# A fused attention, Fourier mix and MLP kernel: two rows of quarter products taken in turn, smaller pieces of w1's operands, and the operands made later

## The chip, the cores and the metric

The kernel runs on one core of one Trainium2 chip. The metric is the device time of one execution in microseconds (us), as the median of several runs; of the kernel before there are three, 1423.19, 1426.36 and 1426.65 us. A traced execution of the same kernel took 1424.23 us, and the traced span from its first to its last instruction is 1422.4 us. All times of stages, waits and instructions are from that one execution.

## The reference

Chunked softmax attention over 8 batches, then a two-dimensional Fourier transform of which the real part is kept, a layer norm, and an MLP with a ReLU between two products:

```python
scores = scale * np.matmul(q_c, k_c.transpose(0, 1, 2, 4, 3))
attn = softmax(scores)                      # per chunk of 64 tokens
x = np.matmul(attn, v_c)                    # bridged to (8, 576, 512)
mixed = np.real(np.fft.fft(np.fft.fft(x, axis=1), axis=2))
u = x + mixed
un = (u - mean) / np.sqrt(var + 1e-06)
out = u + np.maximum(un @ w_ch1, 0.0) @ w_ch2
```

Inputs are q, k and v of 8 x 8 x 576 x 64, w_ch1 of 512 x 2048 and w_ch2 of 2048 x 512, computed in float32. The weights arrive as float64.

## The kernel before

The 4608 tokens are cut into 36 tiles of 128, and these into nine groups of four (`groups`, 512 tokens each): groups 0 to 7 hold the four tiles of one batch, group 8 the leftover chunks of all batches. Each group passes through the MLP as a **first product** (w1, with ReLU into `h1`, 16 rows of 128 features) and a **second product** (w2, with the residual, to the output). The attention and Fourier transform of the next batch run as side work: `side(b)` is a generator, and so is the MLP of a group; the driver at the end (L842 to L866) takes one step `t` of the MLP, then as many steps of the side work as are due by a straight line in `t`. Everything stands in the program in that order (a manual schedule), and each engine works through its own instructions in program order.

Group 0 uses plain products (`mlp_first`, L606): 64 matmuls of 128x512 for each of the two. The groups from 1 on use seven half-size products in place of eight (a Strassen-like scheme, `mlp`, L649): the operands of w1 and w2 are sums and differences of quarters, made once, kept in DRAM as `s1` and `s2` (L95, L96) and streamed back for every group.

- **Making them.** `keep1` (L564) makes four sums of w1's quarters by four GpSimd instructions (L573) into `yall` and stores seven operands with seven DMAs (L576); it is called four times. `keep2` (L578) does it for w2 (L588, L591). The list `conv` (L840, L849) calls one of them per step inside group 0: `keep1` from the step on where more than 16 weight pieces have been rounded, `keep2` once all 32 are through.
- **Rounding.** `load_weight` and `round_weight` (L226 to L258) bring the float64 weights in 32 pieces of 512 KB, 16 of w1 (`wa`) and 16 of w2 (`wb`), and turn each into float32 by four VectorE instructions (L243, L245, L252, L253), three of ScalarE and one of GpSimd (L254).
- **First product, half-size.** One row `m` of eight is a pair of feature blocks. Its seven quarter products (0 to 6, called o0 to o6 below) are two 128x256 matmuls each (L674), into two PSUM tiles `pa` and `pb` of a bank each. After each of them ScalarE (L680, L691) or VectorE (L682, L684, L686, L693, L696) reads the result; the program makes the next product into the same tile wait for that read. `operands(m - 1)` (L659) makes `xs` and `ys` for the second product. The step yields after o3 and after o6.
- **Operands of w1.** `slab1` holds three slabs of 896 KB in `wa`, each with all seven operands of one row. After a row is used, `fetch(1)` (L596, L601) issues the DMA for the row three further on; `fetch(2)` does it for w2's slabs of 1024 KB, one for each quarter product.
- **Second product, half-size.** For each of seven quarter products, two halves of eight matmuls (L727).

Names of the side work: `att_T` transposes q and k (`pt`, L264; ScalarE L274, GpSimd L276 and VectorE L281 write `qT` and `kT`), `att_S` forms scores (`sc`, L293; VectorE L302, L304, L312, L313, L314 and ScalarE L310), `att_P` and `att_V` the weighted sum (`xp`, L331), `fold` and `fourier` the transform (`z`, `mix`). All loads and stores but a few go through SyncE's queue (SP), which issues them in program order and waits there for the engines that they depend on. Each float32 matmul of the program is two records in the trace.

## Time and profile before

| | |
|---|---|
| median of three runs | 1426.36 us |
| the profiled execution, and its span | 1424.23 us, 1422.4 us |
| group 0: first product begins, second begins, group ends | 80.95, 157.43, 298.8 us |
| first product, groups 1 to 8 | 83.4, 83.2, 83.3, 83.2, 83.3, 82.3, 67.6, 67.6 us |
| second product, groups 1 to 8 | 64.9, 66.0, 64.9, 66.0, 65.0, 59.7, 50.1, 53.2 us |

The stages are taken from the first matmul of each on the timeline. Side work runs beside groups 0 to 6; groups 7 and 8 have none in the first product. The lines quoted below have these forms. A group of instructions: line, engine, operation, tiles written and read, sizes, count, then busy time, mean ns of one, and idle time of the engine just before them with what ended it. A timeline row: start, length, engine, instruction, and in brackets the idle time before it with its releaser. A window row: bounds, length, busy time and count of PE, PEld, DVE, ACT and POOL, then the granted TensorE clock, the share of the DMA engines and GB/s. PE is TensorE, PEld its weight load, DVE VectorE, ACT ScalarE, POOL GpSimd, SP SyncE.

### The profile page before, as it was taken

To read this page: it belongs to the slowest core of one execution; us is meant where nothing else is said; L and a number is where in the kernel's file an instruction comes from. 1 tells how busy PE (TensorE), PEld (TensorE's weight loads), DVE (VectorE), ACT (ScalarE), POOL (GpSimd) and SP (SyncE) were. 2 spreads that over 40 slices of the span, in tenths; PEclk is the share of its full clock that TensorE was granted. 3 is DMA by queue.
4 is the path that set the end of the run, shared out by engine and by line. 5 is a ranking of instruction groups with operands and counts; after the bars stand their busy time and mean duration, and the time that the engine had idled before them with its cause. 6 is when DMAs were issued, how large, how long until landed. Compare 5 with 4: busy or idle time off the path is not lost.

```text
span 1422.4 us, 18460 instructions
## 1 busy us (share of the span) xinstructions
PE 1223.7 (86%) x7244; PEld 901.1 (63%) x7244; DVE 587.0 (41%) x1224; ACT 296.3 (21%) x661; POOL 308.6 (22%) x370
## 2 busy tenths in 40 slices
PE   7797348987998889988997899879988998899898
PEld 5443124455687658755785578656865686587577
DVE  4589732444344434434344335432534243313321
ACT  3455511122211211122112211221112101200210
POOL 0338462100330123003200222021303030130121
PEclk9999769999999999999999999999999999999999
DMA  9537665065335433544255425542352234335212
GB/s 214 139 104 222 199 193 127 10 192 191 108 134 171 120 102 110 173 123 134 85 167 150 131 87 140 164 134 89 134 163 83 104 118 141 106 139 174 104 53 95
DMA packets 164028, 189.43 MB, mean 133 GB/s; under 512 B 119461, under 2 KB 137382, under 8 KB 156774
## 3 DMA queue, kind: packets, MB, share of 16 engines
q1 hardware_dynamic: 162150, 187.84, 43.2%
q8 instruction: 57, 0.93, 0.3%
q10 hardware_dynamic: 1600, 0.39, 0.2%
q14 instruction: 29, 0.24, 0.1%
q0 software_dynamic: 192, 0.02, 0.0%
HBM read 163.94 MB, written 24.12 MB: 132 GB/s over the span
## 4 chain that ended last, share of the span: by engine, by line
PE 73%; DVE 13%; ACT 5%; issue 3%; DMA 3%; POOL 3%; SPq 1%; POOLq 0%; ACTq 0%; DVEq 0%
PE pb L674 18%; PE pb L727 16%; PE pa L727 12%; PE pa L674 11%; PE pt L264 4%; PE z L441 3%; PE mix L484 3%; DVE wa L684 2%; DVE h L693 2%; PE dn L625 2%; DVE power L245 2%; DMA xall<-in_moe_w_ch_dram 2%; ACT wa L680 1%; PE xp L331 1%; PE sc L293 1%
## 5 line engine op out<-in xcount | busy, mean ns | idle before, releaser
L663 POOL TENSOR_TENSOR h<-h 128x256 f32<-128x256 f32 x64 | 57.6, 901 | 691.8 <-DVE wb L661 458.3
L674 PE MATMUL pb<-wa 128*128 128x256 f32 x512 | 138.1, 392 | 40.1 <-DVE h L693 40.1
L674 PE MATMUL pb<-unT,wa 128*128 128x256 f32 x512 | 138.1, 392 | 33.1 <-DVE wa L684 33.1
L674 PEld LDWEIGHTS pb<-wa 128*128 128x128 f32 x512 | 92.0, 189 | 75.7 <-DVE h L693 65.8
L674 PE MATMUL pa<-unT,wa 128*128 128x256 f32 x512 | 136.6, 389 | 0.0
L674 PEld LDWEIGHTS pb<-unT,wa 128*128 128x128 f32 x512 | 91.9, 189 | 68.8 <-DVE wa L684 58.8
L727 PE MATMUL pa<-wb,h 128*128 128x256 f32 x512 | 115.6, 381 | 0.0
L727 PE MATMUL pb<-wb,h 128*128 128x256 f32 x512 | 115.1, 381 | 0.0
L674 PE MATMUL pa<-wa 128*128 128x256 f32 x256 | 72.4, 405 | 42.6 <-ACT wa L680 42.6
L727 PEld LDWEIGHTS pa<-wb,h 128*128 128x128 f32 x512 | 95.8, 190 | 16.2 <-issue 3.8
L727 PEld LDWEIGHTS pb<-wb,h 128*128 128x128 f32 x512 | 95.6, 190 | 12.7
L674 PEld LDWEIGHTS pa<-unT,wa 128*128 128x128 f32 x512 | 90.7, 190 | 16.4 <-issue 5.0
L674 PEld LDWEIGHTS pa<-wa 128*128 128x128 f32 x256 | 43.3, 189 | 71.6 <-ACT wa L680 68.3
L682 DVE TENSOR_TENSOR wa<-pa,wa 128x256 f32<-128x256 f32 x64 | 27.2, 424 | 122.4 <-PE pa L674 122.4
L613 PE MATMUL up<-unT,wa 128*128 128x512 f32 x128 | 59.8, 629 | 16.7 <-ACT h L620 15.8
L625 PE MATMUL dn<-wb,h 128*128 128x512 f32 x128 | 63.3, 642 | 0.8 <-ACT h L620 0.8
L691 ACT ACTIVATE h<-pa 128x256 f32<-128x256 f32 x64 | 24.4, 382 | 168.7 <-PE pa L674 168.7
L686 DVE TENSOR_TENSOR h<-pb,wa 128x256 f32<-128x256 f32 x64 | 27.1, 423 | 78.3 <-PE pb L674 78.3
L696 DVE TENSOR_TENSOR h<-pb,wa 128x256 f32<-128x256 f32 x64 | 27.1, 423 | 78.3 <-PE pb L674 78.3
L727 PE MATMUL pa<-wb,yall 128*128 128x256 f32 x256 | 58.2, 381 | 0.0
L727 PE MATMUL pb<-wb,yall 128*128 128x256 f32 x256 | 57.9, 381 | 0.0
L613 PEld LDWEIGHTS up<-unT,wa 128*128 128x128 f32 x128 | 25.7, 203 | 50.3 <-issue 30.6
(148 smaller groups left out, 1818.5 us busy)
## 6 DMA issues: line engine op xcount, KB each, us to landing
wa<-s SPq DMA_DIRECT2D x64, 896.0 KB
wb<-s SPq DMA_DIRECT2D x56, 1024.0 KB
xall<-in_moe_w_ch_dram SPq DMA_DIRECT2D x32, 512.0 KB
v<-in_v_dram SPq DMA_DIRECT2D x142, 64.0 KB
s<-yall SPq DMA_DIRECT2D x32, 256.0 KB
q<-in_q_dram SPq DMA_DIRECT2D x34, 128.0 KB
k<-in_k_dram SPq DMA_DIRECT2D x34, 128.0 KB
q<-in_q_dram SPq DMA_DIRECT2D x14, 256.0 KB
```

What stands on the lines that cost most here:

```text
L245: nc.vector.tensor_scalar(p, hi, 0x7FF00000, None, ALU.bitwise_and)
L264: nc.tensor.transpose(pt[:, j, :], src(j), ident)
L441: nc.tensor.matmul(out=z[:, 0:NQ], lhsT=pm[p, fold_, half], rhs=tk[p, i, fold_, :], start=(i == 0), stop=(i == NM), skip_group_check=(T == 2),
L484: nc.tensor.matmul(out=o[:, cols], lhsT=zt[:, T], rhs=tab, start=(T == 0), stop=(T == 3), skip_group_check=True,)
L613: nc.tensor.matmul(out=up, lhsT=w1[:, kk, m * 128:(m + 1) * 128], rhs=unT[:, kk], start=(kk == 0), stop=(kk == KD - 1),)
L625: nc.tensor.matmul(out=dn, lhsT=h1[:, m, s * 128:(s + 1) * 128], rhs=w2[:, m, :], start=(m == 0), stop=(m == KF - 1),)
L663: nc.gpsimd.tensor_tensor(out=h1[:, m, hi], in0=h1[:, m, lo], in1=h1[:, m, hi], op=ALU.subtract)
L674: nc.tensor.matmul(out=out_, lhsT=w[:, o, kk], rhs=rhs[:, kk], start=(start and kk == 0), stop=(kk == 1), skip_group_check=True,)
L682: nc.vector.tensor_tensor(out=b, in0=pa[:, 1], in1=a, op=ALU.add)
L684: nc.vector.tensor_tensor(out=a, in0=pb[:, 0], in1=b, op=ALU.add)
L693: nc.vector.tensor_tensor(out=h1[:, m, hi], in0=pb[:, 0], in1=b, op=ALU.add)
L727: nc.tensor.matmul(out=dst, lhsT=lhs[:, m], rhs=w[:, m], start=(start and m == 0), stop=(m == HF - 1), skip_group_check=True,)
```

## The change

- **Two rows in turn.** The first product's half-size form (`up_halves`) now takes rows in pairs: o0 of both rows, o1 of both rows, and so on, with `pa` and `pb` for each of the two rows (the same four PSUM banks). It yields after o1, o3, o5 and o6 of a pair, four times as before per two rows. `operands` for the pair before follow o3.
- **Smaller pieces.** `s1` is laid out by pair and quarter product. `slab1` is ten pieces of 256 KB, one for each quarter product of a pair, where it was three slabs of 896 KB; a fetch follows every quarter product. The bytes of a group are the same, in 28 DMAs where there were 8.
- **Operands made later.** `keep1` moves from group 0 to the first eight steps of group 1, `keep2` stays after the last rounded piece; both are generators now, taken three and two small steps per step of the MLP, and `keep1` uses `yall` and `os_` (in `wb`) by turns.
- **Group 1.** Since w1's operands are not there yet, group 1's first product is plain (`up_plain`), with `operands` made behind it; its second product is half-size as before.

```diff
+    s1 = dram.tile([HF // 2, NO, 128, 2 * 2 * 128], FP32, name="s1")
+    NS1, NS2, Z1, Z2 = 10, 3, 2 * 2 * 128, HF * HM
+    slab1 = [wa[:, i * Z1:(i + 1) * Z1].rearrange("p (k r f) -> p k r f", r=2, k=2) for i in range(NS1)]
-    def keep1(f, kk):
+    def keep1(i):
+        f, kk = divmod(i, 2)
...
-        o1, o2, o3, o4 = (yall[:, i] for i in range(4))
+        o1, o2, o3, o4 = ((os_ if i % 2 else yall)[:, j] for j in range(4))
...
             nc.gpsimd.tensor_tensor(out=out_, in0=in0, in1=in1, op=op)
+            yield
+        to = s1.rearrange("a o p (k x) -> p a o k x", k=2)[:, 2 * f:2 * f + 2]
         for o, a in enumerate((a11, o2, o1, o3, a12, o4, a22)):
+            nc.sync.dma_start(out=to[:, :, o, kk], in_=a.rearrange("p (a x) -> p a x", a=2))
+        yield
...
+    first_of = {1: 2, 2: 1}
     def fetch(which):
         i = n_slab[which]
+        if which == 1 and i < HF // 2 * NO * (NG - first_of[1]):
+            pair, o = divmod(i % (HF // 2 * NO), NO)
+            nc.sync.dma_start(out=slab1[i % NS1].rearrange("p k r f -> p (k r f)"), in_=s1[pair, o])
...
+    def up_plain(g):
...
             nc.scalar.activation(out=h1[:, m], in_=up, func=ACTF.Relu)
+            if g >= first_of[2] and m > HF:
+                operands(h1, m - HF - 1)
+            yield h1
...
+    def up_halves(g):
+        rhs = (unT[:, 0:2, lo], tt[:, 1], tt[:, 0], unT[:, 0:2, hi], unT[:, 2:4, lo], unT[:, 2:4, hi], tt[:, 2])
+        for pair in range(HF // 2):
+            pas, pbs = {}, {}
+            for o in range(NO):
+                w = slab1[((g - first_of[1]) * HF // 2 * NO + pair * NO + o) % NS1]
+                for r in range(2):
+                    m = 2 * pair + r
+                    a, b = tmp[:, r, 0], tmp[:, r, 1]
+                    if o == 0:
+                        pas[r] = ps_f.tile([128, 2, 256], FP32, tag="ff", name="pa")
+                    if o == 2:
+                        pbs[r] = ps_f.tile([128, 2, 256], FP32, tag="ff", name="pb")
+                    dst = (pas, pas, pbs, pbs, pas, pbs, pbs)[o][r][:, (0, 1, 0, 1, 0, 0, 1)[o]]
+                    for kk in range(2):
+                        nc.tensor.matmul(
+                            out=dst, lhsT=w[:, kk, r], rhs=rhs[o][:, kk],
+                            start=(o in (0, 2) and kk == 0), stop=(kk == 1), skip_group_check=True,
+                        )
+                    if o == 0:
+                        nc.scalar.copy(a, dst)
+                    elif o == 1:
+                        nc.vector.tensor_tensor(out=b, in0=dst, in1=a, op=ALU.add)
...
+                    elif o == 3:
+                        nc.vector.tensor_tensor(out=h1[:, HF + m, hi], in0=dst, in1=a, op=ALU.add)
+                        if pair > 0:
+                            operands(h1, m - 2)
...
+                fetch(1)
+                if o in (1, 3, 5, 6):
+                    yield h1
...
-                if g == 0 and conv and n_w > (KD * KF // 4 if len(conv) > HF // 2 else len(pieces)):
-                    conv.pop(0)()
+                if n_w > len(pieces):
+                    for _ in range(2):
+                        next(conv2, None)
                 if t == begin[1] - 1:
-                    while conv:
-                        conv.pop(0)()
-                    for _ in range(NS):
+                    for _ in conv2:
+                        pass
+                if begin[1] <= t < begin[1] + KF // 2:
+                    for _ in range(3):
+                        next(conv1, None)
+                if t == begin[1] + KF // 2:
+                    for _ in range(NS2):
+                        fetch(2)
+                if t == begin[1] + KF:
+                    for _ in range(NS1):
                         fetch(1)
```

In the changed file the lines have moved: the first product's matmuls are L690 there, `keep1`'s GpSimd instructions L575, `keep2`'s L592, the rounding's L255.

TensorE at the start of group 2's first product, before (tiles of the program carry numbers, so that the two rows can be told apart):

```order
L674 MATMUL pa_2829<-unT_2570,wa_90 128x256 x2
L674 MATMUL pa_2829<-wa_90 128x256 x2
L674 MATMUL pb_2830<-wa_90 128x256 x2
L674 MATMUL pb_2830<-unT_2570,wa_90 128x256 x2
L293 MATMUL sc_2843<-kT_2746,qT_2739 64x64 x16
L674 MATMUL pa_2829<-unT_2570,wa_90 128x256 x2
L674 MATMUL pb_2830<-unT_2570,wa_90 128x256 x2
L674 MATMUL pb_2830<-wa_90 128x256 x2
L264 MATMUL pt_2881<-ident_81,q_2748 128x128 x4
L264 MATMUL pt_2888<-ident_81,k_2751 128x128 x4
L674 MATMUL pa_2901<-unT_2570,wa_90 128x256 x2
L674 MATMUL pa_2901<-wa_90 128x256 x2
```

The same place in the changed kernel:

```order
L690 MATMUL pa_2716<-unT_2457,wa_90 128x256 x2
L690 MATMUL pa_2720<-unT_2457,wa_90 128x256 x2
L690 MATMUL pa_2716<-wa_90 128x256 x2
L690 MATMUL pa_2720<-wa_90 128x256 x2
L294 MATMUL sc_2732<-kT_2633,qT_2626 64x64 x16
L690 MATMUL pb_2758<-wa_90 128x256 x2
L690 MATMUL pb_2762<-wa_90 128x256 x2
L690 MATMUL pb_2758<-unT_2457,wa_90 128x256 x2
L690 MATMUL pb_2762<-unT_2457,wa_90 128x256 x2
L265 MATMUL pt_2774<-ident_81,q_2635 128x128 x4
L265 MATMUL pt_2781<-ident_81,k_2638 128x128 x4
L690 MATMUL pa_2716<-unT_2457,wa_90 128x256 x2
```

Before, o0 and o1 of a row stand next to each other and write one tile (`pa_2829`); now o0 and o1 of one row (`pa_2716`) have a product of the other row (`pa_2720`) between them, and the step of the side work that forms scores (`sc`) has moved from behind o3 to behind o1.

GpSimd from the last rounded pieces of w1 to the first copies of `qT` of batch 1's attention, before (`yall<-wa` and `yall<-yall,wa` are `keep1`, `yall<-wb` is `keep2`):

```order
L573 TENSOR_TENSOR yall<-wa 128x512
L573 TENSOR_TENSOR yall<-wa,yall 128x512
L254 TENSOR_TENSOR wb<-wb,power 128x512 x11
L588 TENSOR_TENSOR yall<-wb 128x512
L588 TENSOR_TENSOR yall<-wb,yall 128x512
L588 TENSOR_TENSOR yall<-wb 128x512
L588 TENSOR_TENSOR yall<-wb,yall 128x512
L588 TENSOR_TENSOR yall<-wb 128x512
L588 TENSOR_TENSOR yall<-wb,yall 128x512
L588 TENSOR_TENSOR yall<-wb 128x512
L588 TENSOR_TENSOR yall<-wb,yall 128x512
L276 COPY qT<-qT 128x8 x2
```

And in the changed kernel:

```order
L255 TENSOR_TENSOR wa<-wa,power 128x512 x10
L255 TENSOR_TENSOR wb<-wb,power 128x512 x16
L592 TENSOR_TENSOR yall<-wb 128x512
L592 TENSOR_TENSOR yall<-wb,yall 128x512
L592 TENSOR_TENSOR yall<-wb 128x512
L592 TENSOR_TENSOR yall<-wb,yall 128x512
L277 COPY qT<-qT 128x8 x2
L592 TENSOR_TENSOR yall<-wb 128x512
```

The sixteen instructions of `keep1` between the pieces of w2 (four of them in the first rows above) are gone from here, and four instead of eight of `keep2` stand ahead of `qT`.

GpSimd later, in group 1 of the changed kernel, where the same instructions now stand:

```order
L500 TENSOR_TENSOR xall<-y,xall 128x513 x2
L277 COPY qT<-qT 128x8 x2
L575 TENSOR_TENSOR yall<-wa 128x512
L575 TENSOR_TENSOR yall<-yall,wa 128x512
L575 TENSOR_TENSOR yall<-wa 128x512
L350 MEMSET xall 128x1
L575 TENSOR_TENSOR yall<-wa,yall 128x512
L575 TENSOR_TENSOR wb<-wa 128x512
L575 TENSOR_TENSOR wb<-wb,wa 128x512
L575 TENSOR_TENSOR wb<-wa 128x512
L575 TENSOR_TENSOR wb<-wa,wb 128x512
```

The copies of `qT` for batch 2's first tiles stand ahead of `keep1`, and its sums go by turns into `yall` and into `os_` (in `wb`).

More of the change, by code (lines that the diff above doesn't have):

```diff
@@ L582, in keep2 @@
         b21, b22 = w2[:, HF + m:HF + m + 2, 0:HM], w2[:, HF + m:HF + m + 2, HM:DM]
[L583 removed]
+        o1, o2, o3, o4 = (yall[:, j].rearrange("p (m e) -> p m e", m=2) for j in range(4))
         for out_, in0, in1, op in (
@@ L639, in mlp_first @@
                             turned(g + 1, j)
-                            if j >= 2:
+                            if j >= 2 and g + 1 >= first_of[1]:
                                 combined(g + 1, j - 2)
@@ L728, in mlp @@
                         out=dst, lhsT=lhs[:, m], rhs=w[:, m],
-                        start=(start and m == 0), stop=(m == HF - 1), skip_group_check=True,
+                        start=(o in (0, 2) and m == 0), stop=(m == HF - 1), skip_group_check=True,
                     )
@@ L772, in mlp @@
                 yield
+    def mlp(g):
+        for h1 in (up_halves if g >= first_of[1] else up_plain)(g):
+            yield
+        yield from (down_halves if g >= first_of[2] else down_plain)(g, h1)
     with tc.manual_schedule():
@@ L837, with chain @@
         for g in range(NG):
-            begin.append(begin[-1] + (KF + G * PARTS if g == 0 else 2 * HF + 2 * NO))
-        ready_at = [begin[g] + (KF + G * PARTS - 6 if g == 0 else 2 * HF + 4) for g in range(NG)]
-        conv = [lambda f=f, kk=kk: keep1(f, kk) for f in range(2) for kk in range(2)]
-        conv += [lambda i=i: keep2(i) for i in range(HF // 2)]
+            begin.append(begin[-1] + (KF if g < first_of[1] else 2 * HF) + (G * PARTS if g < first_of[2] else 2 * NO))
+        ready_at = [begin[g] + (KF + G * PARTS - 6 if g < first_of[2] else 2 * HF + 4) for g in range(NG)]
+        conv2 = iter([step for i in range(HF // 2) for step in [keep2(i)]])
+        conv1 = iter([step for i in range(4) for step in [keep1(i)]])
+        def chain(gens):
+            for gen in gens:
+                yield from gen
+        conv2, conv1 = chain(conv2), chain(conv1)
         t = 0
         for g in range(NG):
-            for _ in (mlp(g) if g else mlp_first(g)):
+            for _ in mlp(g):
                 t += 1
```

135 lines of the change are left out of this document (50 added, 85 removed).

## The prediction

> **What bounds the kernel now.** I read the page first: its busy times, the granted clock, the chain that ended last, and the groups that waited.
>
> ```profile
> PE 1223.7 (86%) x7244; PEld 901.1 (63%) x7244; DVE 587.0 (41%) x1224; ACT 296.3 (21%) x661; POOL 308.6 (22%) x370
> PEclk9999769999999999999999999999999999999999
> PE 73%; DVE 13%; ACT 5%; issue 3%; DMA 3%; POOL 3%; SPq 1%; POOLq 0%; ACTq 0%; DVEq 0%
> L674 PE MATMUL pb<-unT,wa 128*128 128x256 f32 x512 | 138.1, 392 | 33.1 <-DVE wa L684 33.1
> L674 PE MATMUL pb<-wa 128*128 128x256 f32 x512 | 138.1, 392 | 40.1 <-DVE h L693 40.1
> L674 PE MATMUL pa<-wa 128*128 128x256 f32 x256 | 72.4, 405 | 42.6 <-ACT wa L680 42.6
> ```
>
> TensorE is the bound; no other engine is busy half the time. Its waits in the first product add up to 33.1 + 40.1 + 42.6 = 116 us, each ended by the engine that reads the product before out of the same tile. Next the stages, in windows of the trace.
>
> ```profile
> core 0: us, PE busy (x) PEld busy (x) DVE busy (x) ACT busy (x) POOL busy (x), PEclk, DMA share, GB/s
> 164.00:193.00 29.00, 1.41 (x10) 0.88 (x8) 14.86 (x23) 11.27 (x18) 17.98 (x15) 0.58 0.50 162
> 298.80:382.20 83.40, 68.63 (x507) 49.91 (x501) 35.18 (x79) 20.52 (x44) 13.80 (x23) 1.00 0.53 155
> 447.10:530.30 83.20, 68.71 (x434) 48.66 (x433) 30.70 (x72) 18.58 (x44) 13.64 (x22) 1.00 0.44 131
> 1042.00:1124.30 82.30, 67.80 (x427) 47.77 (x426) 30.02 (x71) 18.00 (x43) 13.62 (x22) 1.00 0.33 109
> 1184.00:1251.60 67.60, 54.79 (x226) 40.57 (x225) 22.28 (x54) 12.99 (x31) 6.26 (x7) 1.00 0.35 119
> 1251.60:1301.70 50.10, 50.10 (x242) 44.12 (x241) 12.05 (x28) 2.54 (x5) 10.09 (x11) 1.00 0.44 153
> ```
>
> These are the startup's hole, the first product of groups 1, 2, 6 and 7, and the second product of group 7. The last two rows say most: the same 112 matmuls of 128x256 take 50.1 us in the second product, with PE busy throughout, and 67.6 us in the first. Side work explains the rest of 83 us: 68.7 - 54.8 = 13.9 us of PE time (13.0 in group 6). The timeline shows one row of group 7, with no side work about.
>
> ```profile
> 1183.98 1.03 PE L674 MATMUL pa<-unT,wa 128*128 128x256 f32 x4
> 1185.52 1.13 PE L674 MATMUL pa<-wa 128*128 128x256 f32 x4 [0.52 <-ACT wa L680]
> 1186.49 1.03 PE L674 MATMUL pb<-wa 128*128 128x256 f32 x4
> 1187.56 0.42 DVE L684 TENSOR_TENSOR wa<-pb,wa 128x256 f32<-128x256 f32 x1 [0.37 <-PE pb L674]
> 1188.04 1.13 PE L674 MATMUL pb<-unT,wa 128*128 128x256 f32 x4 [0.52 <-DVE wa L684]
> 1189.00 1.03 PE L674 MATMUL pa<-unT,wa 128*128 128x256 f32 x4
> 1189.87 1.03 PE L674 MATMUL pb<-unT,wa 128*128 128x256 f32 x4
> 1191.41 1.13 PE L674 MATMUL pb<-wa 128*128 128x256 f32 x4 [0.52 <-DVE h L693]
> 1192.38 1.03 PE L674 MATMUL pa<-unT,wa 128*128 128x256 f32 x4
> ```
>
> From one start to the next is 0.87 us where nothing waits (1189.00 to 1189.87), but 1.54 us at o0-o1, 1.55 at o2-o3 and 1.54 at o5-o6: the product's end 1.03 us after its start, 0.42 us of reading, some 0.1 us of signals. A row takes 1192.38 - 1183.98 = 8.40 us.
>
> **The first product, groups 2 to 8.** With two rows in turn, the product that needs the tile again comes two products later, at 2 x 0.87 = 1.74 us; the reading is through after 1.54 us. The wait is covered with 0.2 us to spare, and the other row's product is the cover; if it fails, the old 0.67 us comes back. A group is then 56 products of 0.87 us, 48.7 us, or 50.1 us by the second product's row; I take 49.5. VectorE has 7 instructions of 0.42 us a row, 3 us of 6.2, so it does not become the bound.
>
> Groups 7 and 8: 67.6 - 49.5 - 0.5 for the last reads = 17.6 us each, **35 us** for both.
>
> In groups 2 to 6 side work stands on VectorE and ScalarE between product and read. Most of its steps hide: their own PE time (0.44 to 0.7 us) plus the product behind is longer than the 0.6 to 0.7 us that they hold VectorE or ScalarE. The exception is the step that forms scores:
>
> ```profile
> 308.54 0.69 DVE L302 TENSOR_REDUCE mx<-sc 128x8 f32<-128x512 f32 x1 [0.23 <-PE sc L293]
> 309.99 0.63 ACT L310 ACTIVATE ex<-ex 128x512 f32<-128x512 f32 x1 [1.02 <-DVE ex L304]
> 310.65 0.69 DVE L312 TENSOR_REDUCE rd<-ex 128x8 f32<-128x512 f32 x1 [0.69 <-ACT ex L310]
> 310.93 1.13 PE L674 MATMUL pa<-wa 128*128 128x256 f32 x4 [1.40 <-ACT wa L680]
> ```
>
> VectorE is held from 308.54 to about 311.8 (two small instructions follow), waiting for ScalarE in the middle. Placed behind o1, as the order shows, the read of o2 starts 3.4 us after that product instead of 1.07, so o3 comes 3.4 + 0.42 + 0.05 - 1.74 = 2.1 us late; behind o3 I get 1.1 us, behind o6 0.9. Two such steps a group: 3.3 us (bounds 0 and 8, the latter if other steps cost 0.4 us each). So a group takes 49.5 + 13.9 + 3.3 = 66.7 us against 83.2, and group 6 65.8 against 82.3: 16.5 each, **82.5 us** for five.
>
> **Group 1's first product** becomes 64 plain matmuls, 128 records.
>
> ```profile
> 80.95 44.87 PE L613 MATMUL up<-unT,wa 128*128 128x512 f32 x104 [0.87 <-DVE unT L533]
> ```
>
> 128 x 44.87 / 104 = 55.2 us, plus 13.9 of side work and some 2 us of waits: 71 against 83.4, **12 us**. Beside it stand `keep1`'s 16 GpSimd instructions and 28 stores. At the 1.25 to 1.7 us that they take on the timeline of before (116 to 147 us) they hold GpSimd some 25 us of the 35 in which they are issued, and the plain product needs only ScalarE. If that cover fails, up to 9 us of the 12 are lost.
>
> **Startup.** Rounding of w2 and, behind it, GpSimd's `qT` hold TensorE:
>
> ```profile
> 111.80 1.40 POOL L254 TENSOR_TENSOR wa<-wa,power 128x512 f32<-128x512 f32 x1 [1.57 <-DVE power L253]
> L254 POOL TENSOR_TENSOR wb<-wb,power x16: 1262/1326/1712, 114.8 to 180.6; 128x512 f32<-128x512 f32 x16
> L243 DVE TENSOR_SCALAR wb<-xall 128x512 uint32<-128x512 uint32 x16 | 14.5, 904 | 10.6 <-DMA xall<-in_moe_w_ch_dram 10.6
> L243 DVE TENSOR_SCALAR wa<-xall 128x512 uint32<-128x512 uint32 x16 | 7.4, 460 | 0.0
> 175.16 1.26 POOL L254 TENSOR_TENSOR wb<-wb,power 128x512 f32<-128x512 f32 x1 [1.90 <-DVE power L253]
> 192.77 0.20 POOL L276 COPY qT<-qT 128x8 f32<-128x8 f32 x1
> 193.03 1.14 PE L293 MATMUL sc<-kT,qT 64*64 64x64 f32 x32 [27.62 <-POOL qT L276]
> 198.64 1.09 PE L264 MATMUL pt<-ident,q 128*128 128x128 f32 x4 [4.48 <-DMA q<-in_q_dram]
> ```
>
> A piece takes 2.97 us before `keep1` begins (1.40 + 1.57) and 3.16 after it has ended (1.26 + 1.90, with fewer buffers for loads), but the sixteen of w2 (the row gives ns, least, median and most, then the first and last start) took 65.8 us; beside `keep1` the same VectorE instruction is twice as long (904 against 460 ns). Without it: 4 x 2.97 + 11 x 3.16 = 46.6, so the last piece starts at 161.4 and not 180.6. Four instructions of `keep2` (1.26 us) instead of eight come before `qT`: 161.4 + 1.3 + 5.0 = 167.7 against 192.8, 25 us sooner. TensorE is there by then: its first product, no longer held, ends near 80.95 + 55.2 = 136. The 4.5 us for q goes too, as the stores of `keep2` no longer stand ahead of that load. The rest of `keep2` now stands among `fold`'s instructions, for which I give back 2.5 us: **27 us** (bounds 15 and 33).
>
> **w1's pieces.** They carry the bytes of before in 2 KB rows, 28 to a group. In 49.5 us that is 7.3 MB, 148 GB/s, and the second product already draws 153. A piece is fetched nine products of a pair ahead, over 15 us.
>
> ```profile
> 284.52 4.48 SPq L601 DMA_DIRECT2D wa<-s  x3
> 285.00:298.00 13.00, 12.27 (x71) 6.21 (x69) 7.16 (x17) 1.85 (x4) 0.23 (x2) 1.00 0.91 280
> 159.27 3.40 DMA xall<-in_moe_w_ch_dram
> ```
>
> Three slabs issued within 4.48 us ran together at 280 GB/s, 0.94 us per 256 KB, so I cost the pieces at nothing. The Trainium skill ("DMA: Bandwidth & Descriptors", section "Measured") advises against this part: "Batch DMAs to ≥1 MiB for ≥75% of peak". By its fit of 2.0 us plus bytes over 436 GB/s (section "Anatomy of one DMA", for another issuing path) a piece alone is an estimated 2.6 us, 73 us for 28, and the sum would be 1424 - 39 - 5 x 10 + 2 x 5 = 1345; that counts only if they do not overlap, and the row of 280 GB/s has transfers overlap. Rival 3 is this mechanism, priced from rows.
>
> The second products keep their work: 0. Sum: 27 + 12 + 82.5 + 35 = 156.5 us from the profiled 1424.2 gives **1268 us**. That execution is 2.1 us under the median of the three runs; I leave it so.
>
> **Rivals.**
>
> 1. *Side work becomes the new wait.* The 0.2 us to spare is thin. If the 13 or so other steps of a group lose 0.7 us each, groups 2 to 6 give 9 us less apiece: 1268 + 45 = 1313. For it: the row at 310.93, where the copy stood behind side work. Against: only the score step holds an engine longer than its cover.
> 2. *The conversion costs the same, later.* `keep1` in group 1 delays `qT` or the loads of q and v by what the startup gains: 1268 + 27 = 1295. Against: its work lies beside 55 us of plain matmuls, and `qT` of batch 2's first tiles stands ahead of it.
> 3. *Slower: pieces come one at a time.* Each waits in SP's queue for the one before. At 3.4 us, the row of a 512 KB load, a first product takes 28 x 3.4 = 95 us: groups 2 to 6 lose 12 us each, 7 and 8 27 us each, and the 39 us elsewhere stay won: 1424 + 60 + 55 - 39 = 1500. It decides from (5 x 83.1 + 2 x 67.6 + 39) / 196 = 3.0 us a piece on. Against: 0.94 us measured together, ten buffers.
>
> **How the numbers follow.** Forecast 0.80, rival 1 0.09, rival 2 0.06, rival 3 0.03, no change 0.02. The forecast's own bounds: startup 15 to 33, group 1 3 to 14, side groups 12 to 19 each, the last two 15 to 19 each; all good ends together give 1244, all bad ends 1316. For 8 in 10 I take 1247 to 1308, which takes in rival 2. About 0.3% is what a measurement of this kernel can tell from no change. Faster by more than that: 0.95; within: 0.02; slower: 0.03.
>
> **What would show it.** Waits of the first product before L680, L684 and L693 fall from 116 us to under 25, the rest standing behind score steps; group 7's first product takes 49 to 51 us, group 2's 64 to 69, group 1's 70 to 73; scores of batch 1 start near 168 us; no PE wait in the first product is ended by a DMA. A row of group 7 with gaps at each product, or DMA as releaser, would prove me wrong.

## The result, and the profile after

The changed kernel takes 1255.66 us, the median of four runs (1253.29 to 1258.09); four runs of the kernel before on the same chip gave 1424.98 us (1423.19 to 1426.65). The ratio is 0.8812, with a 95% interval of 0.8790 to 0.8834. The forecast was 1268 us, with a range from 1247 to 1308. The profiled execution took 1253.29 us, its span 1251.5 us. The stages below are read from one trace of each kernel.

| stage | before, us | after, us | gained | forecast |
|---|---|---|---|---|
| startup: group 0 until group 1 begins, with the head | 298.8 | 272.4 | 26.4 | 27 |
| first product, group 1 | 83.4 | 68.8 | 14.6 | 12 |
| first product, groups 2 to 6 | 83.2, 83.3, 83.2, 83.3, 82.3 | 64.6, 64.9, 64.6, 64.9, 64.6 | 91.7 | 82.5 |
| first product, groups 7 and 8 | 67.6, 67.6 | 48.35, 48.35 | 38.5 | 35 |
| second products, groups 1 to 8, with the tail | 489.8 | 490.1 | -0.3 | 0 |
| sum | | | 171 | 156.5 |

These are the page's lines of the changed kernel that answer to those of before: busy time, the chain that ended last, and the groups of the first product.

```profile
PE 1178.4 (94%) x7148; PEld 895.5 (72%) x7148; DVE 564.6 (45%) x1176; ACT 291.8 (23%) x645; POOL 308.0 (25%) x370
PE 82%; DVE 9%; DMA 3%; ACT 2%; POOL 1%; SPq 1%; issue 1%; ACTq 0%; DVEq 0%; POOLq 0%
L690 PE MATMUL pb<-unT,wa 128*128 128x256 f32 x448 | 106.4, 380 | 8.6 <-DVE wa L699 8.6
L690 PE MATMUL pb<-wa 128*128 128x256 f32 x448 | 108.6, 385 | 1.1 <-DVE h L707 0.9
L690 PE MATMUL pa<-wa 128*128 128x256 f32 x224 | 53.4, 381 | 2.1 <-ACT wa L695 2.1
```

TensorE goes from 86% to 94% of the span. The waits of the first product for a read, 116 us before, are 8.6 + 1.1 + 2.1 = 12 us (with seven groups of this form where there were eight), and no row of the first product is released by a DMA. In the chain that ended last, the share of DVE and ACT falls from 13% and 5% to 9% and 2%. Then the windows, for the first product of groups 1, 2, 7 and 8 (columns as before: bounds, length, busy time of PE, PEld, DVE, ACT and POOL, clock, DMA share, GB/s).

```profile
272.40:341.20 68.80, 68.80 (x411) 33.65 (x405) 21.22 (x39) 15.26 (x28) 30.44 (x36) 1.00 0.75 225
406.10:470.70 64.60, 62.81 (x434) 50.43 (x433) 30.91 (x70) 18.25 (x44) 13.18 (x21) 1.00 0.62 178
1051.20:1099.60 48.40, 48.40 (x226) 42.34 (x226) 21.86 (x52) 13.03 (x31) 5.38 (x6) 1.00 0.57 177
1149.70:1198.00 48.30, 48.30 (x225) 42.28 (x224) 21.85 (x52) 12.98 (x31) 5.38 (x6) 1.00 0.41 132
```

In groups 1, 7 and 8, PE is busy for the whole stage; in group 2, for all but 64.60 - 62.81 = 1.8 us. And the start of group 7 on the timeline, where before o1, o3 and o6 of each row stood behind a gap of 0.52 us:

```profile
1051.24 1.89 PE L690 MATMUL pa<-unT,wa 128*128 128x256 f32 x8
1052.96 1.89 PE L690 MATMUL pa<-wa 128*128 128x256 f32 x8
1054.69 1.89 PE L690 MATMUL pb<-wa 128*128 128x256 f32 x8
1056.42 1.89 PE L690 MATMUL pb<-unT,wa 128*128 128x256 f32 x8
```

A line is one quarter product of both rows, 8 records. From one to the next are 1.73 us, 0.864 us a product, without a gap at o0-o1 or o2-o3.

What is left of the waits stands where the prediction put it, behind the step that forms scores: 1.73 us once in each of groups 2 to 6, and five shorter ones. This is the beginning of group 2:

```profile
411.17 0.69 DVE L305 TENSOR_TENSOR ex<-sc,mx 128x512 f32<-128x512 f32 x1
411.89 0.63 ACT L311 ACTIVATE ex<-ex 128x512 f32<-128x512 f32 x1 [3.46 <-DVE ex L305]
412.55 0.69 DVE L313 TENSOR_REDUCE rd<-ex 128x8 f32<-128x512 f32 x1 [0.69 <-ACT ex L311]
413.60 0.70 DVE L699 TENSOR_TENSOR wa<-pb,wa 128x256 f32<-128x256 f32 x2
414.02 1.99 PE L690 MATMUL pb<-unT,wa 128*128 128x256 f32 x8 [1.73 <-DVE wa L699]
```

VectorE waits 0.69 us for ScalarE's exponential in the middle of the step, sums the row, and only then reads the product that TensorE waits for: 1.73 us.

The startup, on the timeline of GpSimd and TensorE:

```profile
160.49 1.26 POOL L255 TENSOR_TENSOR wb<-wb,power 128x512 f32<-128x512 f32 x1 [0.63 <-DVE power L254]
166.69 0.20 POOL L277 COPY qT<-qT 128x8 f32<-128x8 f32 x1
166.94 1.13 PE L294 MATMUL sc<-kT,qT 64*64 64x64 f32 x32 [21.55 <-POOL qT L277]
210.19 1.26 POOL L592 TENSOR_TENSOR yall<-wb 128x512 f32<-128x512 f32 x1 [5.36 <-DMA s<-yall]
211.66 1.26 POOL L377 TENSOR_TENSOR sum<-xall 128x512 f32<-128x512 f32 x1
213.78 1.33 PE L442 MATMUL z<-tk,pm 128*128 128x289 f32 x2 [9.80 <-POOL pm L388]
```

The last piece is rounded from 160.5 on and the scores of batch 1 start at 166.9, where 161.4 and 167.7 were forecast. New is the end of it: the last round of `keep2` waits at the head of GpSimd's queue for the stores of the round before, the sums of `fold` stand behind it, and TensorE waits 9.80 us for `pm`.

### The profile page after: what moved, and what is told of

Read it like the earlier page. It is cut to its first block, busy times and chain, and to the rows that moved or that the text cites. A ratio compares the mean times of both kernels' runs of the same rounds, so it can differ in the third digit from the quotient of the medians.

```text
span 1251.5 us, 18517 instructions
## 1 busy us (share of the span) xinstructions
PE 1178.4 (94%) x7148; PEld 895.5 (72%) x7148; DVE 564.6 (45%) x1176; ACT 291.8 (23%) x645; POOL 308.0 (25%) x370
## 4 chain that ended last, share of the span: by engine, by line
PE 82%; DVE 9%; DMA 3%; ACT 2%; POOL 1%; SPq 1%; issue 1%; ACTq 0%; DVEq 0%; POOLq 0%
PE pb L737 18%; PE pb L690 15%; PE pa L737 14%; PE pa L690 11%; PE up L626 5%; PE pt L265 5%; PE z L442 4%; PE dn L645 3%; PE mix L485 3%; PE xp L332 2%; PE sc L294 2%; DVE power L246 1%; DMA xall<-in_moe_w_ch_dram 1%; PE idle L816 1%; DVE power L254 1%
## 5 line engine op out<-in xcount | busy, mean ns | idle before, releaser
L626 PE MATMUL up<-unT,wa 128*128 128x512 f32 x256 | 113.9, 597 | 1.8 <-ACT h L633 0.9
L690 PE MATMUL pb<-unT,wa 128*128 128x256 f32 x448 | 106.4, 380 | 8.6 <-DVE wa L699 8.6
L690 PE MATMUL pb<-wa 128*128 128x256 f32 x448 | 108.6, 385 | 1.1 <-DVE h L707 0.9
L690 PE MATMUL pa<-unT,wa 128*128 128x256 f32 x448 | 107.6, 383 | 0.0
L690 PEld LDWEIGHTS pb<-unT,wa 128*128 128x128 f32 x448 | 84.5, 190 | 22.2 <-DVE wa L699 10.7
L690 PEld LDWEIGHTS pb<-wa 128*128 128x128 f32 x448 | 82.2, 190 | 16.2 <-issue 3.4
L690 PEld LDWEIGHTS pa<-unT,wa 128*128 128x128 f32 x448 | 82.5, 190 | 12.0 <-issue 1.2
L626 PEld LDWEIGHTS up<-unT,wa 128*128 128x128 f32 x256 | 47.2, 190 | 56.4 <-issue 52.0
L500 POOL TENSOR_TENSOR xall<-y,xall 128x513 f32<-128x513 f32 x16 | 27.6, 1723 | 128.9 <-DVE y L493 128.9
L737 PE MATMUL pb<-wb 128*128 128x256 f32 x256 | 56.6, 379 | 0.0
L690 PE MATMUL pa<-wa 128*128 128x256 f32 x224 | 53.4, 381 | 2.1 <-ACT wa L695 2.1
L737 PEld LDWEIGHTS pa<-wb,yall 128*128 128x128 f32 x256 | 48.1, 190 | 8.6 <-issue 2.3
L737 PEld LDWEIGHTS pb<-wb 128*128 128x128 f32 x256 | 48.6, 190 | 6.6
```

The source lines that it names most:

```text
L500: eng.tensor_tensor(out=x[:, 0:w], in0=y[:, 0:w], in1=x[:, 0:w], op=ALU.add)
L626: nc.tensor.matmul(out=up, lhsT=w1[:, kk, m * 128:(m + 1) * 128], rhs=unT[:, kk], start=(kk == 0), stop=(kk == KD - 1),)
L690: nc.tensor.matmul(out=dst, lhsT=w[:, kk, r], rhs=rhs[o][:, kk], start=(o in (0, 2) and kk == 0), stop=(kk == 1), skip_group_check=True,)
L737: nc.tensor.matmul(out=dst, lhsT=lhs[:, m], rhs=w[:, m], start=(o in (0, 2) and m == 0), stop=(m == HF - 1), skip_group_check=True,)
```

## The experiments

Each is the changed kernel with the edit shown. The median and range of its runs stand behind it, and the ratio to the kernel before with its 95% interval. Lines are those of the kernel shown.

### One row after the other, small pieces kept

```diff
-            for o in range(NO):
-                w = slab1[...]
-                for r in range(2):
+            for r in range(2):
+                for o in range(NO):
+                    w = slab1[...]
...
-                fetch(1)
-                if o in (1, 3, 5, 6):
-                    yield h1
+                    if r == 1:
+                        fetch(1)
+                    if o in (3, 6):
+                        yield h1
```

> Small pieces and the startup as in the changed kernel, but one row after the other: o0 to o6 of a row, then of the next. Theory (the read of a product is covered by the other row's product): the 0.67 us come back at o1, o3 and o6, groups 7 and 8 take about 67.6 us again and groups 2 to 6 about 83, so the whole is 1256 + 5 x 18.5 + 2 x 19.3 = about 1387 us, and PE waits for L680's, L684's and L693's counterparts are about 100 us again. Rival (the gain of the first product comes from the smaller, more even transfers): it stays within 10 us of 1256.

Measured: 1388.47 us (1384.29 to 1390.40), ratio 0.9736 (0.9715 to 0.9756). The first products of groups 2 to 8 take 83.2, 83.3, 83.2, 84.9, 82.4, 67.6 and 67.6 us, as before the change but for 1.6 us in group 5. The page's groups of this kernel:

```profile
L690 PE MATMUL pb<-wa 128*128 128x256 f32 x448 | 120.8, 392 | 36.0 <-DVE h L707 36.0
L690 PE MATMUL pb<-unT,wa 128*128 128x256 f32 x448 | 120.8, 392 | 29.1 <-DVE wa L699 29.1
L690 PE MATMUL pa<-wa 128*128 128x256 f32 x224 | 63.3, 405 | 36.1 <-ACT wa L695 36.1
```

The 101 us of waits are back, with the small pieces in place and fetched as the second row uses them; no wait of the first product is ended by a DMA. So the turns, and not the pieces, take the waits away; they are worth 133 us. Of these, 101 - 12 = 89 us are waits and 40 us busy time (PE is busy for 1218.5 us on this page, 1178.4 in the changed kernel, for the same 7148 records): a product that the next one doesn't follow at once counts for longer, as the mean of 405 ns against 381 in the last line shows. The edit puts the side work back behind o3 and o6 as well, but groups 7 and 8 have none there and lose their 19.2 us each all the same.

### Two rows in turn, w1's operands in slabs of a row

```diff
-    s1 = dram.tile([HF // 2, NO, 128, 2 * 2 * 128], FP32, name="s1")
-    NS1, NS2, Z1, Z2 = 10, 3, 2 * 2 * 128, HF * HM
+    s1 = dram.tile([HF, 128, NO * 2 * 128], FP32, name="s1")
+    NS1, NS2, Z1, Z2 = 3, 3, NO * 2 * 128, HF * HM
...
-                fetch(1)
+                if o == NO - 1:
+                    fetch(1)
+                    fetch(1)
```

> Two rows in turn, but w1's operands in three slabs of 896 KB, one for each row, as before the change; both rows of a pair give their slab back only at the pair's end. Theory: the waits for the reads stay away (under 25 us), but the second slab of the next pair is asked for when the pair ends and needed 0.87 us later; at 280 GB/s it takes 3.3 us and some 1 to 2 us to start, so 4 to 5 us at each pair but a group's first, 21 x 4.5 = 95 us: about 1350 us, the waits ended by a DMA. Rival (the size of the pieces does not matter for taking rows in turn): within 10 us of 1256.

Measured: 1373.47 us (1370.98 to 1380.22), ratio 0.9649 (0.9616 to 0.9681): 118 us more than with the pieces. First the page's busy times and the waits by line and releaser (us in total, times, longest), then one of them on the timeline of group 8, then the windows of the 3 us in it and of the 3.4 us behind:

```profile
PE 1217.0 (89%) x7148; PEld 919.0 (67%) x7148; DVE 563.4 (41%) x1176; ACT 292.3 (21%) x645; POOL 304.0 (22%) x370
PE pa L689 <- DMA wa<-s: 79.6, 21, 9.7
```

```profile
1152.61 1.03 PE L689 MATMUL pa<-unT,wa 128*128 128x256 f32 x4
1156.55 1.18 PE L689 MATMUL pa<-unT,wa 128*128 128x256 f32 x4 [2.92 <-DMA wa<-s]
1157.53 3.54 PE L689 MATMUL pa<-wa 128*128 128x256 f32 x8
1160.90 1.89 PE L689 MATMUL pb<-wa 128*128 128x256 f32 x8
```

```profile
1153.50:1156.50 3.00, 0.13 (x1) 0.00 (x0) 0.00 (x0) 0.66 (x2) 0.00 (x0) 1.00 0.94 378
1157.50:1160.90 3.40, 3.40 (x9) 2.66 (x8) 0.42 (x1) 0.37 (x1) 0.00 (x0) 0.51 0.12 49
```

Two rows in turn use two slabs at a time and give both back at the end of a pair; with three slabs the second row of each next pair is fetched only then. 21 waits (three pair changes in each of seven groups) make 79.6 us. The products run slower too: PE is busy for 1217.0 - 1178.4 = 38.6 us more than in the changed kernel, for the same records. These two make the 118 us. The second is the clock for the most part: behind the wait shown, 8 records take from 1157.53 to 1160.90, 3.37 us instead of 1.73, at a granted clock of 0.51, and 20 of the 21 waits have such a stretch at or behind them. The first row of a new pair has no wait, and the reads hold TensorE as little as in the changed kernel. So the theory was right in kind. It priced the waits too high (21 x 4.5 = 95 us) and left out the clock, so that its 1350 us came out 23 us too low. The rival (the size does not matter) falls. Startup and group 1 make 41 of the 169 us gained; beyond them turns without pieces are worth some 10 us, pieces without turns nothing, and both together 128.

### Pieces of 128 KB

```diff
-    NS1, NS2, Z1, Z2 = 10, 3, 2 * 2 * 128, HF * HM
+    NS1, NS2, Z1, Z2 = 20, 3, 2 * 128, HF * HM
```

`s1` is laid out by row and quarter product, and a fetch follows each product.

> The changed kernel, with w1's operands fetched in pieces of one row (128 KB, 1 KB per partition, 20 buffers, 392 fetches) instead of two rows (256 KB, 2 KB per partition, 10 buffers, 196 fetches). Bytes and memory stay the same. Theory: far enough ahead of their use the pieces cost nothing, however small: a piece of 128 KB is used up in 0.86 us and 20 of them are 17 us ahead, as 10 larger ones are now: 1256 us, the groups without side work stay at 48.4 us, no TensorE wait in the first product is ended by a DMA. Rival: each fetch has a price of its own, and at one per 0.86 us the queue falls behind: TensorE then waits for wa in the first products, and the groups without side work grow in proportion, for a fetch per 1.2 us to 56 x 1.2 = 67 us, and the whole by some 2 x 19 + 5 x 5 = 63 us, to 1320.

Measured: 1254.00 us (1252.62 to 1255.39), ratio 0.8797 (0.8778 to 0.8817), the same as with 256 KB, as the theory has it; the rival's 1320 us falls. The window of group 7's first product:

```profile
1051.11:1099.40 48.29, 48.29 (x225) 42.27 (x224) 21.85 (x52) 12.97 (x31) 5.38 (x6) 1.00 0.59 181
```

Twice the fetches, half the length of a row in memory, and PE is busy throughout; the share of the DMA engines is 0.59 at 181 GB/s where it was 0.57 at 177.

### Two buffers for the pieces

```diff
-    NS1, NS2, Z1, Z2 = 10, 3, 2 * 2 * 128, HF * HM
+    NS1, NS2, Z1, Z2 = 2, 3, 2 * 2 * 128, HF * HM
```

> The changed kernel with 2 buffers for w1's pieces instead of 10, so that hardly any fetch is ahead of its use and the time L of one 256 KB piece from issue to landing shows itself: a buffer comes free when its two products are read, and its next piece is there L later, while one other piece (1.73 us of products) is used up. The pitch of pieces becomes the larger of 1.73 us and (L + 1.73)/2. Theory: L is some 3.4 us, so a piece taken strictly one at a time is dearer than its products, and only the 10 buffers hide it: pitch 2.57 us, groups without side work 28 x 2.57 = 72 us instead of 48.4, groups with side work some 10 to 12 us longer since the side work between the products gives the pieces time: about 1256 + 2 x 24 + 5 x 11 = 1359 us. Rival: a piece lands in 1.7 us or less after its issue, and two buffers are enough: 1256 to 1262 us. If L is 2.6 us: pitch 2.17, 61 us, about 1310.

Measured: 1431.54 us (1423.60 to 1437.95, ten runs), ratio 1.0041 (1.0018 to 1.0065): all of the gain is gone, where the theory had 1359 us. The waits of TensorE, and the start and a stretch of group 8:

```profile
PE pb L690 <- DMA wa<-s: 90.7, 52, 9.1
PE pa L690 <- DMA wa<-s: 37.2, 34, 5.6
```

```profile
1318.17 3.75 PE L690 MATMUL pb<-wa 128*128 128x256 f32 x8 [7.71 <-DMA wa<-s]
1343.47 1.97 PE L690 MATMUL pb<-unT,wa 128*128 128x256 f32 x8 [0.55 <-DMA wa<-s]
1345.83 1.97 PE L690 MATMUL pb<-wa 128*128 128x256 f32 x8 [0.40 <-DMA wa<-s]
1348.25 1.96 PE L690 MATMUL pa<-unT,wa 128*128 128x256 f32 x8 [0.45 <-DMA wa<-s]
1350.52 1.97 PE L690 MATMUL pa<-wa 128*128 128x256 f32 x8 [0.31 <-DMA wa<-s]
```

Groups 7 and 8 take 77.1 and 74.0 us (72 were expected). In the stretch shown a piece is used every 2.36 us (1343.47 to 1350.52 are three). With two buffers that is half the sum of L and the 1.73 us of products, so L is some 2 x 2.36 - 1.73 = 3.0 us from the buffer coming free to the use of the next piece. That makes 28 x 2.36 = 66 us of group 8's stage; the other 8 us are the wait of 7.71 us at its start. Each of the seven first products has such a wait, of 5.7 to 9.1 us, and the theory has no term for it. That its 72 us are near for groups 7 and 8 is luck: L was put too high (3.4), and the start was left out. For groups 2 to 6 the size was wrong: these take 85 to 92 us, 25 more, where 11 were expected. Besides the wait at the start, the side work gives no time for the pieces, because its loads and stores stand in SP's queue between the fetches. In group 2 this queue issues the first lines below, and the last is what TensorE then meets:

```profile
415.87 13.87 SPq L606 DMA_DIRECT2D wa<-s  x4
429.85 1.37 SPq L167 DMA_DIRECT2D q<-in_q_dram  x2
432.68 5.67 SPq L606 DMA_DIRECT2D wa<-s  x3
438.69 2.58 SPq L177 DMA_DIRECT2D v<-in_v_dram  x4
441.38 1.15 SPq L360 DMA_DIRECT2D first<-xall  x2
```

```profile
448.51 3.46 PE L690 MATMUL pb<-wa 128*128 128x256 f32 x8 [5.44 <-DMA wa<-s]
```

From 429.85 to 432.68 and from 438.69 on (until 445.56) no piece is issued, while two buffers hold 3.5 us of products. So the price of a fetch is there, and it is the distance of ten buffers that hides it. The rival (two buffers are enough) falls.

### Operands made in group 0, group 1 half-size

```diff
-    first_of = {1: 2, 2: 1}
+    first_of = {1: 1, 2: 1}
```

The driver calls `keep1` and `keep2` in group 0 as in the kernel before; alternation and pieces stay.

> Rows in turn and small pieces kept; w1's operands made inside group 0 again, all four sums and seven stores in one step, and group 1's first product half-size. Theory: the startup's 26.4 us come back (scores of batch 1 start near 193 us, group 0 ends near 299 us), group 1's first product takes 64.8 us in place of 68.8, the rest stays: 1256 + 26.4 - 4 = 1278 us. Rival (making the operands costs the same wherever it stands): 1252 us, since only the cheaper first product of group 1 is left.

Measured: 1273.79 us (1271.57 to 1275.40), ratio 0.8934 (0.8918 to 0.8950), 18 us more than the changed kernel. On the timeline:

```profile
193.11 1.14 PE L294 MATMUL sc<-kT,qT 64*64 64x64 f32 x32 [27.59 <-POOL qT L277]
198.54 1.09 PE L265 MATMUL pt<-ident,q 128*128 128x128 f32 x4 [4.30 <-DMA q<-in_q_dram]
```

Group 0 lasts 215.6 us from its first product on, 24.5 more than in the changed kernel, with the scores at 193.1 and the wait for q as they were before; group 1's first product takes 63.1 us, 5.6 less than the plain one. By the stages the later operands are worth 24.5 - 5.6 = 19 us, by the medians 18 (22 by the theory): the startup term holds, and the rival (making them costs the same wherever it stands, 1252 us) falls.

### The row sums of a score step at the end of the next step

```diff
         nc.scalar.activation(out=ex, in_=ex, func=ACTF.Exp, scale=scale)
+        es[n] = ex
+
+    def att_R(n):
+        ex = es[n]
         rd = sm_p...
...
                 att_T(n + 1)
+            att_R(n)
             yield
```

> The changed kernel, with the score step cut in two: maximum, subtraction and exponential stay in it, the row sum, the addition and the reciprocal (L313 to L315) move to the end of the next step. Theory (the score step holds VectorE for 3.3 us, over the cover of 1.74): VectorE is now held about 1.5 us, the waits of the first product for L699 fall from 19 us to under 5, groups 2 to 6 go from 64.7 to about 62.7 us each, the whole to about 1246 us. Rival (the hold only moves to the next step, where it meets the same margin of 0.2 us): within 3 us of 1256.

Measured: 1249.25 us (1247.08 to 1251.67), ratio 0.8763 (0.8747 to 0.8780). The group of this kernel that waited most in the changed one (L704 is the L699 there):

```profile
L695 PE MATMUL pb<-unT,wa 128*128 128x256 f32 x448 | 106.8, 381 | 1.5 <-DVE wa L704 1.5
```

The wait behind the score step falls from 8.6 to 1.5 us, and groups 2 to 6 take 62.9, 64.4, 62.9, 64.4 and 61.7 us, 7.3 less in all. So most of the remaining waits were the second half of the score step: VectorE's stop for the exponential and the row sum behind it. The rival (the hold only moves) falls. The 19 us that the expectation names for L699 are the waits of TensorE's matmuls and of its weight loads added up; the matmuls' own were 8.6. Group 0 came out 3 us longer here, which need not be a result of the edit: from the first product to the beginning of group 1, the changed kernel and three others with the same group 0 took 191.1, 189.8, 190.0 and 190.1 us, and one with the same took 194.3, as this did (194.2).

### The startup: the column of qT on ScalarE, and the last round of `keep2` later

Two edits, apart and together. The first takes the copy that the scores wait for from GpSimd's queue; the second lets the last round of `keep2` run only when batch 1's Fourier part is issued.

```diff
-            nc.gpsimd.tensor_copy(t[:, :, 0:1], t[:, :, CH:CH + 1])
+            if tiles[n][1] == 1:
+                nc.scalar.copy(t[:, :, 0:1], t[:, :, CH:CH + 1])
+            else:
+                nc.gpsimd.tensor_copy(t[:, :, 0:1], t[:, :, CH:CH + 1])
```

```diff
-                        next(conv2, None)
+                        if cur > 0 or n_2 < 3 * 5:
+                            next(conv2, None)
+                            n_2 += 1
```

> The changed kernel, with the copy of one column of qT for the tiles of batch 1 on ScalarE instead of GpSimd. In the changed kernel the first scores of batch 1 wait for that copy until 166.9 us, because on GpSimd it stands behind all the rounding (until 161.7) and the first four steps on w2's operands (until 166.7). Expected of both theories: the wait of 21.55 us before the scores ends some 5 us earlier or more, by 162 us, unless something else is late there. Theory A (GpSimd's queue behind the operands' stores sets the end of the startup): the last of the four operand steps still starts at 210 us, the sums of the second tile pair stand behind it, so the Fourier products' wait of 9.8 us grows by what was gained before: within 2 us of 1256. Theory B (the column alone holds the startup): the 5 us come through, 1250 us.

Measured: 1250.17 us (1245.37 to 1251.94), ratio 0.8763 (0.8739 to 0.8786).

> The changed kernel, with the last of the four rounds on w2's operands held back until batch 1's Fourier part is issued (its four steps and seven stores come later, none is left out). In the changed kernel that round stands on GpSimd at 205 us, waits 5.36 us for the stores of the round before, and the sums of the second tile pair (211.4 to 214.4) stand behind it: TensorE waits 9.80 us for pm there. Theory A: without the round ahead the sums start when x is there (204.1) and end by 207.2, the wait falls from 9.8 to about 3.3 us, group 1 begins some 6.5 us earlier: 1249 us. Rival: something else is late there (the rows that are shifted by DMA, the ScalarE's eviction of zr, a later place for the same round), and the wait moves: within 2 us of 1256.

Measured: 1247.56 us (1246.89 to 1247.77), ratio 0.8749 (0.8735 to 0.8763).

> The changed kernel with both edits of the startup: the column of qT of batch 1 on ScalarE, and the last round of steps on w2's operands behind batch 1's Fourier part. Alone they gave 5.5 us (of which group 0's stages show 3.6, the wait for pm having grown from 9.8 to 11.7 us) and 8 us (6.9 in group 0's second product). Theory A (the same queue of GpSimd sets both waits, so that what the first edit gains was partly held by the second place): together more than the sum of what group 0 shows apart, 10.5 to 13 us: 1243 to 1245 us, the wait for pm below 4 us. Rival (they are the same few us, found twice): not below 1247 us.

Measured, both edits: 1240.16 us (1238.87 to 1242.15), ratio 0.8705 (0.8691 to 0.8719). The scores and the Fourier products on the three timelines: first with qT on ScalarE, then with the later round, then with both.

```profile
162.83 1.13 PE L297 MATMUL sc<-kT,qT 64*64 64x64 f32 x32 [15.88 <-DVE kT L285]
211.99 1.33 PE L445 MATMUL z<-tk,pm 128*128 128x289 f32 x2 [11.70 <-POOL pm L391]
```

```profile
168.26 1.13 PE L294 MATMUL sc<-kT,qT 64*64 64x64 f32 x32 [21.70 <-POOL qT L277]
209.90 1.33 PE L442 MATMUL z<-tk,pm 128*128 128x289 f32 x2 [3.47 <-POOL pm L388]
```

```profile
160.84 1.13 PE L297 MATMUL sc<-kT,qT 64*64 64x64 f32 x32 [15.91 <-DVE kT L285]
202.75 1.09 PE L445 MATMUL z<-tk,pm 128*128 128x289 f32 x2 [2.60 <-POOL pm L391]
```

The later round does what theory A said: the wait for `pm` falls to 3.47 us and group 0 lasts 184.3 us (190 to 194 without it); the rival, by which the wait moves, falls. The column alone brings the scores 5.8 us forward, counted from the first product, and leaves 187.4 us, and the median is theory B's 1250 (theory A had 1256); whether its gain was partly held at `pm` (11.7 us now) is not settled, since that wait was 9.8 to 11.8 us in kernels with the same column and rounds. Both together give 180.2 us and 15.5 us less than the changed kernel. The rival (the same few us found twice) falls, and the time is below theory A's range too. That the pair brings more than the sum of the two (5.5 and 8.1) is not shown, the difference being within the 4 us by which group 0 varies.

### All three edits

> The same, and in addition the row sums, the 1e-6 and the reciprocal of each attention step at the end of the next step, as in the run that gave 1249.25 us (groups 2 to 6 shorter by 8.5 us in all, group 0's second product longer by 3). Theory: the gains lie in different stages and add: 1244 less 8.5 plus up to 3 gives 1236 to 1239 us, faster than every kernel before it. Rival: the later sums hold back the shortened startup by more than 3 us (they stand in VectorE's queue between the rounding and the next scores): 1240 us or more.

Measured: 1233.63 us (1230.98 to 1235.82, five runs), ratio 0.8658 (0.8642 to 0.8674), under the range given and faster than every other kernel here. The page's busy times:

```profile
PE 1177.3 (96%) x7148; PEld 895.2 (73%) x7148; DVE 566.8 (46%) x1176; ACT 291.6 (24%) x647; POOL 307.9 (25%) x368
```

The same PE work as in the changed kernel (1178.4 us) in 21 us less span. Groups 2 to 6 are as with the row sums moved alone, and group 0 lasts 176.5 us: the later sums do not hold back the startup.

## Why the prediction was right, and where its sizes were off

- **TensorE as the bound, its waits behind reads of the same tile.** Shown: undoing the turns brings these waits back, 101 us of them, and the old stage lengths with them.
- **The cover of 0.2 us.** It holds. In groups 7 and 8 no product waits, and the read of one row lies wholly behind the other row's product.
- **Groups 7 and 8: 17.6 us each forecast, 19.25 measured.** The mechanism is right, the term mis-sized: 49.5 us was taken as the middle of 48.7 and 50.1, plus 0.5 for last reads. The products run at 0.864 us each, 56 x 0.864 = 48.4, and the last reads lie beside the second product. The lower bound was the better value, since the second product's 50.1 us had other work of PE in it: its row counts 242 records, and the 224 of the MLP make 48.4.
- **Groups 2 to 6: 82.5 forecast, 91.7 measured.** Of the 9.2 us, 1.15 a group is the same base (49.5 against 48.35), and some 0.9 us a group the score steps: 3.3 us were put on them, and TensorE waits 1.8 to 2.8 us a group, 2.4 in the mean. (Some 0.2 us a group go the other way, as TensorE is busy with side work for a little longer than forecast.) The step behind o1 was sized nearly right (2.1 forecast, 1.73 measured). Those behind o3 and o6, put at about 1 us each, were not: the step behind o3 costs nothing in groups 2 and 4 and 0.9 us in group 6, the one behind o6 0.5 us in groups 3 and 5.
- **Group 1: 12 forecast, 14.6 measured.** 55.2 + 13.9 = 69.1 against 68.8 measured; the 2 us put on waits did not come, and GpSimd's 30.4 us beside it did not hold TensorE, which is busy for the whole stage.
- **Startup: 27 forecast, 26.4 measured, but by terms that offset each other.** That the two agree to 0.6 us is luck, since group 0 alone varies by 4 us between traces. The end of the rounding, the copy of `qT` and the end of the first product came as forecast (160.5, 166.7 and 137.5 us against 161.4, 167.7 and 136), and the wait for q at that place went. The term that failed is "I give back 2.5" for the rest of `keep2` among the `fold` instructions. The wait for `pm` there is 9.80 us where it was 0.39 + 3.98 = 4.4 before, so 5.4 us were given back, and holding one round of `keep2` back takes 6.3 of the 9.80 away. The prediction gives no working for its 2.5, and it does not name what the runs show: a round waits at the head of the queue for the stores of the round before (5.36 us). Against that the scores came 26.1 us sooner (193.03 to 166.94), 1 us more than the 25 forecast; 26.1 + 4.5 for q - 5.4 is 25.2, and 1.2 us lie spread over the rest of group 0. One reading ahead of the sum was wrong, though the sum does not use it: the VectorE instruction at L243 was called twice as long beside `keep1` (904 against 460 ns), but in the changed kernel, with `keep1` gone from there, the same instruction (L244) still takes 811 ns on the pieces of w2 and 459 on those of w1.
- **The pieces: nothing, as forecast.** No wait is ended by one, at 256 KB or 128 KB. The rate of the transfers did not decide: slabs of 896 KB moved at 378 GB/s in the wait shown, pieces at 177 over group 7, where nothing waited for them. The slabs cost 118 us more because they are given back late. The Trainium skill ("DMA: Bandwidth & Descriptors", "Measured") says to batch DMAs to at least 1 MiB for 75% of the peak rate, measured there for DMAs that GpSimd issues; no run here tells the rate of a transfer by its size, and the time went the other way than that rule would have it. By the fit of the same page ("Anatomy of one DMA") a piece alone is an estimated 2.6 us; two buffers show 3.0 us from a buffer coming free to the use of its next piece.
- **The rivals.** The first (side work as the new wait, 1313) has 12 us of waits for it in all, where the rival put 45 on top of those forecast. The second (the conversion costs the same later, 1295) is ruled out by the run with the operands in group 0. The third (pieces one at a time, 1500) is a real mechanism: with two buffers it costs 176 us. It decided nothing because ten buffers stand ahead.

## What to carry to other kernels

When an engine waits for another to read its result out of a tile, put independent work of the same length between the two uses, and compare the pitch of that work with the whole reading chain; here 0.2 us to spare was enough for 133 us. Then ask what the new order needs at one time: two rows in turn need two rows of operands, and in the memory at hand it was smaller pieces, each given back as soon as it was used, that kept the fetches ahead of the products. A conversion that is moved into a queue costs what its instructions wait for at the head of it, not what they are busy, so look for what stands behind each of them.

## What the runs showed of the hardware that was not expected

- TensorE's granted clock was 0.51 for 3.4 us behind a wait of 2.92 us (with slabs of 896 KB), which made that wait half as dear again; with waits of 0.3 to 0.6 us (two buffers, the stretch of group 8 shown) it stayed at 1.00. The length of the wait alone does not decide: with the same slabs a wait of 2.02 us that ended at 425.90 us was followed by a clock of 0.50 (426.99 to 430.40), and one of 3.12 us that ended at 1043.33 by a clock of 1.00. In the twelve traces here the clock changes only on a grid of steps of 3.41 us, and the step just past decides: at full clock, all 91 steps in which TensorE was busy for at most 0.41 of the step were followed by half clock, and none of the 4114 in which it was busy for more than 0.55. The wait of 2.02 us lies within one step (423.58 to 426.99, 1.39 us busy); the one of 3.12 us is split by the line at 1041.39, with 2.23 us busy in the step before and 1.47 in the step behind. The Trainium skill ("TensorE: Matmul & The Clock Gate", "What's actually happening") says that the clock is halved after an idle window of some 3.4 us and comes back after a busy one of as long. The 0.51 and the 3.4 us agree with that; here shorter waits were enough, where they fell within one step.
- 392 fetches of 128 KB in rows of 1 KB and 196 of 256 KB in rows of 2 KB gave the same time of the kernel and took nearly the same share of the DMA engines in group 7 (0.59 at 181 GB/s, 0.57 at 177).
- SP's queue took some 0.6 us for each DMA in the rows shown (two in 1.15 us, four in 2.58), so that with two buffers ten loads and stores of the side work kept the next fetch back for 6.9 us (438.69 to 445.56).
- Kernels with an identical group 0 differ there by 4 us (190 or 194), so edits of the startup below that size need several runs.
